# The fourth conv group of a conv + RWKV channel-mix kernel: x instead of the Toeplitz matrix as the stationary operand

## The chip, the cores and the metric

One core of a Trainium2 chip. The metric is the time of one execution on the device, in microseconds (us). Engines: PE (TensorE: matmuls, and PEld, its weight loads), DVE (VectorE), ACT (ScalarE), POOL (GpSimd) and SP (SyncE, DMA issue). PSUM is the memory that matmuls write; SBUF is the one that all engines and DMA use.

## The reference, cut to what matters

A causal 7-tap convolution along the sequence, one set of softmaxed taps for each of 8 heads of 24 channels, and then the RWKV channel mix on its output y (8 sequences of 4160 tokens, 192 channels, d_ff 1024):

```python
# convolution: w = softmax(weight) per head, x padded with 6 zero rows in front
out = np.einsum('hk,bskhg->bshg', w, x_unf)
# channel mix, on x = out
x_prev = np.concatenate([np.zeros((B, 1, D), dtype=np.float32), x[:, :-1, :]], axis=1)
xk = mu_k * x + (1.0 - mu_k) * x_prev
xr = mu_r * x + (1.0 - mu_r) * x_prev
k = np.maximum(xk @ w_k, 0.0)
v = k * k @ w_v
r = 1.0 / (1.0 + np.exp(-(xr @ w_r)))
return (r * v).astype(np.float32)
```

## The kernel before, in words

The sequences are worked in four pairs. The channel mix wants y with channels on the partitions: tile yT, 128 partitions of 3 channel thirds of 64 channels, the pair's two sequences one above the other. The convolution of a block of tokens is a matmul with a banded Toeplitz matrix of a head, `toe[:, h, :]`, built from the taps at the start.

The channel mix runs in steps of 512 tokens of a pair (the first of 256). Each step has d = y - y_prev, xk and xr on DVE (lines 530 to 571), then for each 128 columns of d_ff one *slot*: k_mm (six matmuls into a PSUM tile of two banks, line 591), k_relu on ACT into k_sb (line 603), k_square on DVE into k2 (line 617). Four slots make a *bundle*. Later r (line 648), r_out (a sigmoid on ACT, line 659), v_rows (64 matmuls with wv in two halves, line 679) and v_out (r times v on DVE, line 695, then stored by SP) finish 256 tokens.

All PSUM is one ring of four tiles of two banks, tag "k": the k tiles, ps_r, ps_v and the convolution's tiles (ps_c, ps_t) take turns, and a new one waits until the engine that reads the oldest free one is done. After the first v half a `clobber_nop` stands on ACT, which lets the second half write the banks in the other order.

The order is written out by hand: every engine runs its instructions in the order of the code (`manual_schedule`). The first bundles have a function each: `bundle_first` (bundle 0), `bundle_second` (1), `bundle_third` (2); from bundle 3 on `bundle_rest`. Tables (early, mix_a, mix_b, mix_c, late, xt and so on) name what else runs in a bundle.

The convolution of pair 0 has six groups of tokens. Groups 0, 1 and 2 (3, 4 and 4 blocks of 120 tokens) are done by `conv_t`: x is the stationary operand in 128x32 tiles (126 tokens with their halo by up to 32 channels), `toe` is the moving one with 120 columns, so the result stands with channels on the partitions, and one copy, `to_yT`, takes it to yT. A tile of 32 channels touches two heads, so each (sequence, 32 channels) has two matmuls, the second over the narrower piece. Group 3 (5 blocks, tokens 1320 to 1919; its x is called x3 here) goes another way. In bundle 1 `conv_mm` makes two units of eight matmuls, `toe` stationary in 64x128 tiles; `conv_out` casts them from PSUM into y (tokens on the partitions), the first unit in bundle 1, the second in bundle 2; and in bundle 3 `tr` turns y by 15 transposes with an identity matrix on PE, into two PSUM tiles, from which DVE makes three copies into yT. Groups 4 and 5 of pair 0 and all groups of the other pairs write y to DRAM and read it back with a transposing DMA.

x is loaded by POOL's DMA queue, which casts to bf16: the weights wk, wr and wv come by the same queue. x3 and group 0 to 2 share one buffer `xb`, which group 6 takes over at the head of bundle 3: a small memset on DVE (line 123) waits until the old tile is free, then POOL sets rows to zero (line 125) and issues the loads. POOL also makes the identity `ident` (`select_equal`) in the prologue, between the loads of group 2 and of group 3.

Of the kernel before, what the change touches and what calls it, by code (L numbers as in the profile page):

```python
# [7 lines left out]
FP32 = mybir.dt.float32  # L8
BF16 = mybir.dt.bfloat16
# [5 lines left out]
def kernel(  # L15
# [23 lines left out]
    GB = 10  # L39
# [4 lines left out]
    BANK = 512  # L44
# [3 lines left out]
    YC = 16  # L48
# [31 lines left out]
    n = 0  # L80
# [108 lines left out]
    ident = const.tile([P, P], BF16)  # L189
# [78 lines left out]
    def select_equal(t, n):  # L268
        nc.gpsimd.affine_select(
            out=t,  # L270
            in_=(ones_t if t is ident else ones6)[0:n, 0:n],
            pattern=[[1, n]],
            compare_op=ALU.is_equal,
            fill=0.0,
            base=0,
            channel_multiplier=-1,
        )
# [94 lines left out]
    def conv_units(g):  # L372

        return [((0, 1), (6, 7)), ((2, 3), (4, 5))]

    def conv_mm(g, c, half):

        nb = groups[g][2]
        if half == 0:
            if c == 0:  # L380
                ys[g] = two.tile([P, GB, 2 * D], BF16, tag="y", name="y")
            conv_ps[g, c] = ring.tile([P, 2, BANK], FP32, tag="k", name="ps_c")
        unit = conv_units(g)[c]
        last = len(unit[0]) - 1
        banks = conv_ps[g, c][:, :, 0 : nb * 2 * G * (last + 1)].rearrange("p i (n s c) -> p i n s c", n=nb, s=2)
        for k in range(last + 1):
            for i in range(2):
                q = slice(i * Q, (i + 1) * Q)
                bank = (i + half) % 2
                h = unit[bank][k]  # L390
                nc.tensor.matmul(
                    out=banks[:, bank, :, :, k * G : (k + 1) * G],
                    lhsT=toe[q, h, :],
                    rhs=xbs[g][q, :nb, :, h * G : (h + 1) * G],
                    start=half == 0 and k == 0,
                    stop=half == 1 and k == last,
                )
        if half == 0:
            nc.scalar.clobber_nop([nc.scalar.lower_ap(conv_ps[g, c])])

    def conv_t(g, c, o, blocks):

        for n, i in enumerate(blocks):
            for first_piece in (True, False):
                for s in range(2):
                    for q in range(2):
                        c0 = c * Q + q * 32
                        lo, hi = c0 // G, (c0 + 31) // G
                        h, m = (hi, 32) if first_piece else (lo, hi * G - c0)
                        p0 = s * Q + q * 32  # L410
                        nc.tensor.matmul(  # L411
                            out=o[p0 : p0 + m, n * BLK : (n + 1) * BLK],
                            lhsT=xbs[g][:, i, s, c0 : c0 + m],
                            rhs=toe[:, h, 0:BLK],
                            start=True,
                            stop=True,
                        )

# [3 lines left out]

    def conv_out(g, c, copy):

        nb = groups[g][2]
        unit = conv_units(g)[c]
        w = G * len(unit[0])
        ps = conv_ps.pop((g, c))[:BLK, :, :]
        y = ys[g][:BLK, :, :]
        parts = []  # L430
        for hs in unit:
            c0, c1 = hs[0] * G, (hs[-1] + 1) * G
            cuts = [c0] + [a for a in range(Q, D, Q) if c0 < a < c1] + [c1]
            parts.append(sorted((b - a, a - c0, a // Q * 2 * Q + a % Q) for a, b in zip(cuts, cuts[1:])))
        for (n, s0, d0), (m, s1, d1) in zip(*parts):
            assert n == m and d1 > d0
            copy(
                out=bass.AP(
                    tensor=y.tensor,
                    offset=y.offset + d0,  # L440
                    ap=[y.ap[0], [d1 - d0, 2], [2 * D, nb], [Q, 2], [1, n]],
                ),
                in_=bass.AP(
                    tensor=ps.tensor,
                    offset=ps.offset + s0,
                    ap=[ps.ap[0], [BANK + s1 - s0, 2], [2 * w, nb], [w, 2], [1, n]],
                ),
            )
# [41 lines left out]

    def tr(g, j):

        p, base, nb, _, _ = groups[g]
        ps = ring.tile([P, 2, 2 * BANK], BF16, tag="k", name="ps_t")
        todo = range(4 * j, min(nb, 4 * j + 4))
        view = ps[:, :, 0 : 6 * BLK].rearrange("p b (c i t) -> p b c i t", c=3, i=2)
        for i0 in todo[::2]:
            for c in range(3):
                for i in range(i0, min(nb, i0 + 2)):
                    nc.tensor.transpose(  # L500
                        out=view[:, (i - 4 * j) // 2, c, i % 2, :],
                        in_=ys[g][:BLK, i, c * P : (c + 1) * P],
                        identity=ident[:BLK, :BLK],
                    )

        for i in todo[::2]:
            n = min(2, nb - i)
            c0 = YC + base + i * BLK
            nc.vector.tensor_copy(
                out=yTs[p][:, :, c0 : c0 + n * BLK].rearrange("p c (n t) -> p c n t", n=n),  # L510
                in_=view[:, (i - 4 * j) // 2, :, :n, :],
            )
# [223 lines left out]
    def conv_half(unit, half):
        if unit is not None:
            conv_mm(*unit, half)
            if half == 1:
                conv_out(*unit, nc.scalar.copy)  # L740

    for g, (p, base, nb, fb, on_pe) in enumerate(groups):
        if g < 3:
            continue
        if p == 0:
            xs = {3: [1, 1], 4: [2, 2, 3, 3], 5: [4, 4, 5, 5]}[g]
# [4 lines left out]
        if not on_pe:  # L751
            at(late, xs[-1], y_write, g)
# [10 lines left out]
        if not on_pe:  # L763
            if g == 4:
                at(mix_c, 4, y_read, g, slice(0, 1), 2)
                at(late, 4, y_read, g, slice(1, 2), 2)
            else:
                at(late, 6, y_read, g)
# [54 lines left out]
    def prologue():  # L823
# [38 lines left out]
        select_equal(ident, P)  # L862
# [7 lines left out]
    def bundle_first(ns):  # L870
        new_yT(0)
        tiles = [ring.tile([P, 2, BANK], FP32, tag="k", name="ps_t") for _ in range(2)]
        for n, (g, c) in enumerate((g, c) for g in range(2) for c in range(NC)):
            o = tiles[n % 2][:, n // 2 % 2, :]
            conv_t(g, c, o, range(groups[g][2]))
# [24 lines left out]
    def bundle_second(b, ns):  # L900
# [15 lines left out]
        conv_t(g, 2, outs[2], range(4))  # L916
# [14 lines left out]
    def bundle_rest(b, ns):  # L931
# [3 lines left out]
        if b == 3:  # L935
# [3 lines left out]
            tr(3, 0)  # L939
            tr(3, 1)  # L940
# [42 lines left out]
    def bundle_third(b, ns):  # L983
# [13 lines left out]
        conv_out(*xt[b - 1][1], nc.scalar.copy)  # L997
# [67 lines left out]
```

## Time and profile before

| | us |
|---|---|
| three runs | 411.59, 412.29, 415.82 |
| median | 412.29 |
| span of the profiled execution, first to last instruction | 409.5 |
| sixteen conv matmuls of group 3 start (bundle 1) | 18.74 |
| first v pass starts (bundle 2) | 22.60 |
| fifteen transposes start (bundle 3) | 27.94 |

No time of its own is listed for the profiled execution beside its span; the median of the runs is 2.8 us longer than that span.

In a row of the timeline stand start, length, engine, line, operation, out<-in, the shape of the tile and of the data, and the count of merged instructions. Matmuls are pipelined, so lengths of neighbouring groups overlap and the difference of two starts is what a group takes. In brackets is the time that the engine was idle before, and what ended it. "issue" means that the profile shows nothing that was waited for.

### The profile page before, as it was taken

The page shows a single profiled execution, that of the slowest core. Times are in us where ns is not written, and L with a number is a line of the kernel's source. Part 1 is how long each engine was busy: PE and PEld are TensorE (multiplying, and loading weights), DVE is VectorE, ACT ScalarE, POOL GpSimd, SP SyncE. Part 2 cuts the span into 40 slices and gives each one's busy share as a digit, 9 for nine tenths or more (in the row PEclk, how much of TensorE's full clock was granted, in tenths as well). Part 3 has the DMA queues.
Part 4 walks back from the last instruction along what each step waited for, and adds up shares of the span by engine and source line. Part 5 has one row for each costly group of instructions (what it writes and reads, how often), then busy time and mean ns, then how long its engine had stood idle before and what let it go on. Part 6 is the DMA issues. An engine that isn't in the chain of part 4 may idle for free.

```text
span 409.5 us, 17547 instructions
## 1 busy us (share of the span) xinstructions
PE 401.2 (98%) x7736; PEld 302.2 (74%) x7736; DVE 370.4 (90%) x672; ACT 354.6 (87%) x426; POOL 56.8 (14%) x91
## 2 busy tenths in 40 slices
PE   8899999999999999999999999999999999999996
PEld 5567777777877767777776777777777778777795
DVE  5999898988999989999999999999999899999973
ACT  6899989989888989988898998889899878877781
POOL 8622202200230202004020022000000000000000
PEclk9999999999999999999999999999999999999999
DMA  9999999997399998789995996977623856221223
GB/s 148 188 201 207 197 204 192 213 249 179 90 203 264 193 193 134 158 212 178 205 141 151 236 170 132 171 176 206 121 91 89 209 135 157 80 71 48 80 80 115
DMA packets 138955, 66.23 MB, mean 162 GB/s; under 512 B 89356, under 2 KB 138880, under 8 KB 138880
## 3 DMA queue, kind: packets, MB, share of 16 engines
q1 hardware_dynamic: 95536, 48.20, 46.9%
q0 software_dynamic: 42544, 16.36, 34.8%
q8 instruction: 60, 0.98, 0.9%
q10 hardware_dynamic: 800, 0.57, 0.5%
q14 instruction: 15, 0.12, 0.1%
HBM read 33.29 MB, written 36.86 MB: 171 GB/s over the span
## 4 chain that ended last, share of the span: by engine, by line
PE 92%; DMA 4%; POOL 1%; DVE 1%; ACT 1%; issue 1%; POOLq 0%; DVEq 0%
PE ps_v L679 41%; PE ps_k L591 39%; PE ps_r L648 8%; PE ps_c L362 2%; DMA xb<-in_x_dram 2%; DMA wk<-in_moe_w_k_dram 2%; PE ps_v L631 1%; ACT k_sb L603 1%; PE ps_c L317 0%; POOL wk L224 0%; POOL xb L152 0%; DVE k L617 0%; DVE yT L421 0%; DVE o_sb L695 0%; POOL tap L258 0%
## 5 line engine op out<-in xcount | busy, mean ns | idle before, releaser
L603 ACT ACTIVATE k_sb<-ps_k 128x1024 bf16<-128x1024 f32 x260 | 253.3, 1038 | 34.9 <-PE ps_k L591 33.8
L617 DVE TENSOR_TENSOR k<-k_sb 128x1024 bf16<-128x1024 bf16 x260 | 173.6, 688 | 26.1 <-ACT k_sb L603 25.8
L591 PE MATMUL ps_k<-xk,wk 64*128 64x512 bf16 (+1 forms) x1632 | 192.0, 367 | 1.5 <-DMA wk<-in_moe_w_k_dram 1.3
L679 PE MATMUL ps_v<-wv,k 64*128 64x192 bf16 x4032 | 188.5, 243 | 0.5 <-DMA wv<-in_moe_w_v_dram 0.5
L679 PEld LDWEIGHTS <-k 64*128 64x128 bf16 x4032 | 168.2, 94 | 13.1 <-issue 4.6
L591 PEld LDWEIGHTS <-wk 64*128 64x128 bf16 x1632 | 83.6, 94 | 56.9 <-issue 2.0
L695 DVE TENSOR_TENSOR o_sb<-ps_v,r_sb 128x768 f32<-128x768 f32 x64 | 60.9, 951 | 2.6 <-issue 2.4
L152 POOL DMA_DIRECT2D xb<-in_x_dram x62 | 43.5, 708 | 131.8 <-DVE xb L111 59.8
L659 ACT ACTIVATE r_sb<-ps_r 128x768 bf16<-128x768 f32 x65 | 53.4, 824 | 7.9 <-PE ps_v L679 5.7
L335 ACT CAST y<-ps_c 128x960 bf16<-128x960 f32 (+2 forms) x84 | 52.6, 708 | 0.0
L648 PEld LDWEIGHTS <-xr 64*128 64x128 bf16 x780 | 35.0, 94 | 14.8 <-issue 1.0
L648 PE MATMUL ps_r<-wr,xr 64*128 64x192 bf16 x780 | 43.4, 243 | 0.3 <-issue 0.3
L565 DVE TENSOR_SCALAR xr<-d,mu 128x512 bf16<-128x512 bf16 (+1 forms) x102 | 35.2, 349 | 0.0
L565 DVE TENSOR_SCALAR xk<-d,mu 128x512 bf16<-128x512 bf16 (+1 forms) x99 | 32.5, 358 | 0.1
L534 DVE TENSOR_TENSOR d<-yT 128x1536 bf16<-128x1536 bf16 (+4 forms) x36 | 31.2, 867 | 1.2 <-ACT yT L421 1.1
L571 DVE TENSOR_TENSOR xr<-xr,yT 128x1536 bf16<-128x1536 bf16 (+1 forms) x33 | 31.1, 941 | 1.1
L571 DVE TENSOR_TENSOR xk<-xk,yT 128x1536 bf16<-128x1536 bf16 (+3 forms) x33 | 30.5, 925 | 0.1
L518 POOL COPY y_tail<-yT 128x195 bf16<-128x195 bf16 x4 | 2.8, 690 | 89.1 <-DMA yT<-y_dram 89.1
L362 PEld LDWEIGHTS <-toe 32*32 32x32 bf16 x768 | 4.9, 87 | 10.2 <-issue 8.7
L362 PE MATMUL ps_c<-xb,toe 32*32 32x240 bf16 x768 | 10.7, 267 | 0.0
L125 POOL MEMSET xb<- 32x384 bf16 x3 | 1.2, 407 | 67.1 <-DVE xb L123 67.1
L411 PE MATMUL ps_t<-toe,xb 128*32 128x120 bf16 (+3 forms) x264 | 5.4, 234 | 0.3 <-ACT yT L421 0.2
(60 smaller groups left out, 61.8 us busy)
## 6 DMA issues: line engine op xcount, KB each, us to landing
out_dram<-o_sb SPq DMA_DIRECT2D x128, 192.0 KB
xb<-in_x_dram POOLq DMA_DIRECT2D x52, 240.0 KB, 8.1
y_dram<-y SPq DMA_DIRECT2D x48, 195.0 KB
y_dram<-y SPq DMA_DIRECT2D x8, 210.0 KB
xb<-in_x_dram POOLq DMA_DIRECT2D x6, 228.0 KB, 4.7
xb<-in_x_dram POOLq DMA_DIRECT2D x4, 192.0 KB, 6.5
wk<-in_moe_w_k_dram POOLq DMA_DIRECT2D x4, 192.0 KB, 6.2
wv<-in_moe_w_v_dram POOLq DMA_DIRECT2D x1, 384.0 KB, 10.1
```

What stands on the lines that cost most here:

```text
L152: nc.gpsimd.dma_start(out=xb[q0 : q0 + rows, lo:hi, s, :], in_=bass.AP(tensor=x.tensor, offset=x.offset + (b * S + t0 + lo * step) * D, ap ...
L335: nc.scalar.copy(out=bass.AP(tensor=y.tensor, offset=y.offset + d, ap=[y.ap[0], [m * 2 * D, 2], [2 * D, m], [Q, 2], [1, b - a]],), in_=bas ...
L534: nc.vector.tensor_tensor(out=shaped(s, diffs[s][:, cs, :L]), in0=y_of(s, cs, 1), in1=y_of(s, cs, 0), op=ALU.subtract)
L565: nc.vector.tensor_scalar(out=t[:, c, :L], in0=diffs[s][:, c, :L], scalar1=mu[:, i, c : c + 1], scalar2=None, op0=ALU.mult)
L571: nc.vector.tensor_tensor(out=o, in0=o, in1=y_of(s, sl, 0), op=ALU.add)
L591: nc.tensor.matmul(out=ps[:, i, f * L : (f + 1) * L], lhsT=wk[r, c, fs], rhs=xk[r, c, :L], start=c == 0 and f == 0, stop=c == NC - 1 and f ...
L603: nc.scalar.activation(out=k_sb, in_=ps.rearrange("p a b -> p (a b)"), func=AF.Relu)
L617: nc.vector.tensor_tensor(out=o, in0=i, in1=i, op=ALU.mult)
L648: nc.tensor.matmul(out=ps[:, i, k * D : (k + 1) * D], lhsT=xr[q, c, ts], rhs=wr[q, c, :], start=c == 0, stop=c == NC - 1,)
L659: nc.scalar.activation(out=r_sbs[s, j], in_=r_ps.pop((s, j))[:, :, 0 : 2 * D], func=AF.Sigmoid)
L679: nc.tensor.matmul(out=v_ps[s, j][:, bank, k * D : (k + 1) * D], lhsT=k2s[s][q, f, t * P : (t + 1) * P], rhs=wv[q, f, :], start=half == 0 ...
L695: nc.vector.tensor_tensor(out=o_sb.rearrange("p (b t) d -> p b (t d)", b=2), in0=v_ps.pop((s, j)), in1=r_sbs.pop((s, j)), op=ALU.mult,)
```

## The change

Group 3 is done by `conv_t` too. It takes a list of pieces (block, first column, end column) instead of blocks. The new `conv_t5` does one channel third of five blocks: two and a half blocks into each of a PSUM tile's two banks, the third block in halves of 60 columns, and one cast of 600 columns into yT, by ACT for thirds 0 and 1 and by DVE for third 2. Third 0 runs in bundle 1, third 1 in bundle 2 behind the first v pass, third 2 in bundle 3 where the transposes were. `conv_units`, `conv_mm`, `conv_out`, `conv_half`, `tr` and `ident` go.

```diff
-        select_equal(ident, P)
...
+    def conv_t(g, c, o, pieces):
+
+        at = 0
+        for i, t0, t1 in pieces:
...
-                            out=o[p0 : p0 + m, n * BLK : (n + 1) * BLK],
+                            out=o[p0 : p0 + m, at : at + t1 - t0],
                             lhsT=xbs[g][:, i, s, c0 : c0 + m],
-                            rhs=toe[:, h, 0:BLK],
+                            rhs=toe[:, h, t0:t1],
                             start=True,
                             stop=True,
                         )
+            at += t1 - t0
...
+    def conv_t5(g, c, copy):
+
+        ps = ring.tile([P, 2, BANK], FP32, tag="k", name="ps_t")
+        h = BLK // 2
+        conv_t(g, c, ps[:, 0, :], [*whole(2), (2, 0, h)])
+        conv_t(g, c, ps[:, 1, :], [(2, h, BLK), (3, 0, BLK), (4, 0, BLK)])
+        c0 = YC + groups[g][1]
+        copy(
+            out=yTs[0][:, c, c0 : c0 + 5 * BLK].rearrange("p (b t) -> p b t", b=2),
+            in_=ps[:, :, 0 : 5 * h],
+        )
...
         run(mix_a, b)
-        conv_half(xt[b][0], 0)
         k_relu(ns[3])
-        conv_half(xt[b][0], 1)
+        conv_t5(3, 0, act_)
         k_square(ns[1])
         run(mix_b, b)
-        conv_mm(*xt[b][1], 0)
-        conv_mm(*xt[b][1], 1)
         run(mix_c, b)
...
-            tr(3, 0)
-            tr(3, 1)
+            conv_t5(3, 2, nc.vector.tensor_copy)
...
         v_rows(*quad, 0)
-        conv_out(*xt[b - 1][1], nc.scalar.copy)
+        conv_t5(3, 1, nc.scalar.copy)
         k_square(ns[1])
```

How it moves instructions. PE in bundle 2, at the end of the first v pass: before, the k pass follows at once.

```order
L679 LDWEIGHTS k_504
L679 MATMUL ps_v<-wv,k_504 128x192
L591 LDWEIGHTS wk
L591 MATMUL ps_k<-xk,wk 128x512 [waits Activation_49]
L591 LDWEIGHTS wk
```

Now the 48 matmuls of third 1 start there, with x as the weights (the line numbers are those of the changed kernel).

```order
L616 LDWEIGHTS k_502
L616 MATMUL ps_v<-wv,k_502 128x192
L382 LDWEIGHTS xb
L382 MATMUL ps_t<-toe,xb 32x120 [waits Activation_49]
L382 LDWEIGHTS xb
```

The k pass stands behind all 48; in bundle 1 the sixteen ps_c matmuls are gone, and 48 of these stand in the place of the first four.

ACT in bundles 1 and 2 before: the relu of bundle 1's last slot, the cast of the first unit, two relus, the sigmoid, the second unit's two casts.

```order
L603 ACTIVATE k_sb<-ps_k 128x1024 [waits DVE_49,Activation_49,PE_49]
L437 CAST y<-ps_c 120x2x5x2x48 [waits Activation_sequencer_49,PE_49]
L603 ACTIVATE k_sb<-ps_k 128x1024 [waits Activation_49,PE_49,DVE_49]
L603 ACTIVATE k_sb<-ps_k 128x1024 [waits DVE_49,PE_49]
L659 ACTIVATE r_sb<-ps_r 128x768 [waits PE_49]
L437 CAST y<-ps_c 120x2x5x2x16 [waits Activation_49,PE_49,Activation_sequencer_49]
L437 CAST y<-ps_c 120x2x5x2x32
```

And now:

```order
L540 ACTIVATE k_sb<-ps_k 128x1024 [waits PE_49,Activation_49]
L401 CAST yT<-ps_t 128x600 [waits PE_49]
L540 ACTIVATE k_sb<-ps_k 128x1024 [waits DVE_49,PE_49] x2
L596 ACTIVATE r_sb<-ps_r 128x768 [waits PE_49]
L401 CAST yT<-ps_t 128x600 [waits DVE_49,Activation_49,PE_49]
```

Three casts into y have become two into yT, at the same places among the relus.

DVE at the head of bundle 3 before: v_out of bundle 2, the memset that takes the old x buffer for group 6, the three copies of the transposes, two squares.

```order
L695 TENSOR_TENSOR o_sb<-ps_v,r_sb 128x768 [waits Activation_sequencer_49,PE_49,Activation_49]
L123 MEMSET xb 1x1 [waits DMASW6_49,DMASW7_49,DMASW1_49,DMASW0_49]
L509 COPY yT<-ps_t 128x3x240 [waits PE_49]
L509 COPY yT<-ps_t 128x3x240
L509 COPY yT<-ps_t 128x3x120 [waits PE_49]
L617 TENSOR_TENSOR k_644<-k_sb 128x1024 [waits Activation_49] x2
```

And now:

```order
L632 TENSOR_TENSOR o_sb<-ps_v,r_sb 128x768 [waits Activation_sequencer_49,PE_49,Activation_49]
L123 MEMSET xb 1x1 [waits DMASW6_49,DMASW1_49,DMASW7_49,DMASW0_49,PE_49]
L401 CAST yT<-ps_t 128x600
L554 TENSOR_TENSOR k_642<-k_sb 128x1024 [waits Activation_49] x2
L502 TENSOR_SCALAR xr<-d,mu 128x512 x3
```

The memset has gained a wait for PE, since third 2 is the last reader of x3, and the cast behind it needs no wait of its own any more.

More of the change, by code (lines that the diff above doesn't have):

```diff
@@ L188 @@
     ones_t = const.tile([P, P], BF16)
-    ident = const.tile([P, P], BF16)
     w_nrm = const.tile([32, 32], BF16)
@@ L270, in select_equal @@
             out=t,
-            in_=(ones_t if t is ident else ones6)[0:n, 0:n],
+            in_=ones6[0:n, 0:n],
             pattern=[[1, n]],
@@ L370, in conv_sparse @@
             cast_tiles(y, ps, m, c)
[L372 to L403, printed above, removed]
+    def conv_t(g, c, o, pieces):
+        at = 0
+        for i, t0, t1 in pieces:
             for first_piece in (True, False):
@@ L417, in conv_t, with whole @@
                         )
+            at += t1 - t0
+    def whole(n):
+        return [(i, 0, BLK) for i in range(n)]
+    def conv_t5(g, c, copy):
[8 more added lines that the diff above has]
+        )
     def to_yT(g, c, o, b0, b1, copy):
@@ L421, in to_yT @@
         copy(out=yTs[0][:, c, c0 : c0 + (b1 - b0) * BLK], in_=o[:, 0 : (b1 - b0) * BLK])
[L423 to L448, printed above, removed]
     def new_yT(p):
@@ L488, in y_read @@
         )
[L491 to L512, printed above, removed]
     diffs, xks, xrs = {}, {}, {}
@@ L734, in at @@
         table.setdefault(b, []).append((fn, a))
[L736 to L740, printed above, removed]
     for g, (p, base, nb, fb, on_pe) in enumerate(groups):
-        if g < 3:
+        if g < 4:
             continue
         if p == 0:
-            xs = {3: [1, 1], 4: [2, 2, 3, 3], 5: [4, 4, 5, 5]}[g]
+            xs = {4: [2, 2, 3, 3], 5: [4, 4, 5, 5]}[g]
         else:
@@ L750 @@
             xt.setdefault(b, []).append((g, i))
-        if not on_pe:
-            at(late, xs[-1], y_write, g)
+        at(late, xs[-1], y_write, g)
         if g in sparse:
@@ L762 @@
             continue
[L763 to L768, printed above, removed]
+        if g == 4:
+            at(mix_c, 4, y_read, g, slice(0, 1), 2)
+            at(late, 4, y_read, g, slice(1, 2), 2)
+        else:
+            at(late, 6, y_read, g)
         if g > 4:
@@ L874, in bundle_first @@
             o = tiles[n % 2][:, n // 2 % 2, :]
-            conv_t(g, c, o, range(groups[g][2]))
+            conv_t(g, c, o, whole(groups[g][2]))
             if n == 0:
@@ L908, in bundle_second @@
         outs = [tiles[0][:, 0, :], tiles[1][:, 0, :], tiles[0][:, 1, :]]
-        conv_t(g, 0, outs[0], range(4))
+        conv_t(g, 0, outs[0], whole(4))
         to_yT(g, 0, outs[0], 0, 4, dve_)
         k_relu(ns[1])
-        conv_t(g, 1, outs[1], range(4))
+        conv_t(g, 1, outs[1], whole(4))
         to_yT(g, 1, outs[1], 0, 4, dve_)
@@ L915, in bundle_second @@
         k_relu(ns[2])
-        conv_t(g, 2, outs[2], range(4))
+        conv_t(g, 2, outs[2], whole(4))
         to_yT(g, 2, outs[2], 0, 4, act_)
```

## The prediction

> **What bounds the kernel now.** I read the page first (busy time per engine), then stretches of the span, then TensorE's waits, then the timeline of bundles 1 to 3, where all changed instructions lie. The page's first part, and four stretches (each engine's busy us, granted clock, busy share of the DMA engines, GB/s):
>
> ```profile
> PE 401.2 (98%) x7736; PEld 302.2 (74%) x7736; DVE 370.4 (90%) x672; ACT 354.6 (87%) x426; POOL 56.8 (14%) x91
> ...
> 18.50:22.60 4.10, 3.37 (x44) 2.04 (x41) 4.07 (x9) 3.95 (x6) 2.16 (x4) 1.00 1.59 191
> 22.60:29.40 6.80, 6.64 (x114) 4.77 (x115) 6.18 (x13) 6.01 (x9) 1.40 (x3) 1.00 1.59 192
> 29.40:46.00 16.60, 16.58 (x308) 11.95 (x311) 16.33 (x31) 16.06 (x22) 4.05 (x7) 1.00 1.18 215
> ```
>
> TensorE is the bound from 22.6 us on (6.64 of 6.80, 16.58 of 16.60 us), at a granted clock of 1.00. Before that it is not: 3.37 of 4.10 us. DVE and ACT run close behind it up to 46 us. TensorE's waits from 29 us to the end:
>
> ```profile
> PE ps_r L648 <- issue: 0.3, 1, 0.3
> PE ps_k L591 <- issue: 0.2, 1, 0.2
> PE ps_c L317 <- ACT k_sb L603: 0.2, 1, 0.2
> ```
>
> 0.7 us in 380. So a delay of TensorE at 29 us is a delay of the end: no idle time is left to absorb it. The timeline of TensorE in bundles 1, 2 and 3 (start, length, what, count; bracketed, the idle time before it and its releaser):
>
> ```profile
> 15.73 1.02 PE L411 MATMUL ps_t<-toe,xb 128*32 128x120 bf16 x64
> 16.80 0.82 PE L591 MATMUL ps_k<-xk,wk 64*128 64x512 bf16 x6
> 17.55 0.60 PE L411 MATMUL ps_t<-toe,xb 128*32 128x120 bf16 x32
> 18.09 0.82 PE L591 MATMUL ps_k<-xk,wk 64*128 64x512 bf16 x6
> 18.74 1.52 PE L391 MATMUL ps_c<-xb,toe 64*128 64x240 bf16 x16
> 20.09 1.47 PE L591 MATMUL ps_k<-xk,wk 64*128 64x512 bf16 x12
> 21.38 0.68 PE L648 MATMUL ps_r<-wr,xr 64*128 64x192 bf16 x12
> 22.60 1.49 PE L679 MATMUL ps_v<-wv,k 64*128 64x192 bf16 x32 [0.55 <-DMA wv<-in_moe_w_v_dram]
> 23.93 0.81 PE L591 MATMUL ps_k<-xk,wk 64*128 64x512 bf16 x6
> 24.58 0.82 PE L679 MATMUL ps_v<-wv,k 64*128 64x192 bf16 x16
> ...
> 26.55 1.46 PE L591 MATMUL ps_k<-xk,wk 64*128 64x512 bf16 x12
> 27.94 0.96 PE L500 MATMUL ps_t<-ident,y 120*128 120x120 bf16 x15
> 28.83 0.40 PE L317 MATMUL ps_c<-xb,toe 64*64 64x240 bf16 x8
> 29.39 0.40 PE L317 MATMUL ps_c<-xb,toe 64*64 64x240 bf16 x8 [0.16 <-ACT k_sb L603]
> 29.81 0.82 PE L591 MATMUL ps_k<-xk,wk 64*128 64x512 bf16 x6
> ```
>
> The reader is to take differences of starts, since the lengths overlap: 16 v matmuls cost 0.66 us, a k pass of six 0.65, the 15 transposes 0.89. The one real wait lies at 22.60: the first v pass needs wv, and TensorE stands 0.55 us for its transfer. Work taken off TensorE ahead of that point buys nothing; work added behind it is paid in full.
>
> **The change, part by part.** First the price of one new convolution: 48 matmuls in 128x32 tiles, 32 of them 120 columns wide and 16 of them 60. The same instruction with 120 columns stands in the timeline: 64 take 1.07 us (15.73 to 16.80), 32 take 0.54 (17.55 to 18.09), so 16.8 ns each, with no fixed part. The 60-column form does not occur before. Its bounds are no saving (16.8 ns) and half (8.4 ns), so a channel third costs 0.67 to 0.81 us; the nearest rows decide for neither end, and I take the middle, 0.74. Entering the narrow tiles costs a little: the k pass ahead of them steps 0.75 us (16.80 to 17.55) against 0.65 ahead of a v pass, so 0.10; leaving them costs nothing that shows.
>
> The page "TensorEngine Tiling (Array Packing)" of the Trainium skill (Instruction Overhead) puts about 60 cycles under each matmul, so that 60 columns would not yet be padded; by it the 60-column form costs half and a third 0.67 us. Its section Key Properties says that a change of tiling mode drains the array, which speaks against this change, as it adds one such excursion in bundle 2; the trace agrees that there is a cost and makes it 0.10 us.
>
> *Bundle 1, the sixteen L391 matmuls (both units) replaced by one third:* 1.35 us (18.74 to 20.09) goes, 0.74 + 0.10 comes: TensorE is 0.51 us earlier at 22.60, where it now stands about 1.06 us for wv instead of 0.55. On the path: 0, hidden by that wait; were the wait gone, it would be worth its 0.51. Whether wv can come earlier depends on POOL and the DMA:
>
> ```profile
> 8.27 0.37 POOL L269 TENSOR_SCALAR_AFFINE_SELECT ident<-ones_t 128x128 bf16<-128x128 bf16 x1
> ...
> 12.20 0.93 POOL L237 DMA_DIRECT2D wv<-in_moe_w_v_dram  x1 [0.34 <-DMA wk<-in_moe_w_k_dram]
> ...
> 22.57 0.71 POOL L152 DMA_DIRECT2D xb<-in_x_dram  x1 [1.84 <-DMA wv<-in_moe_w_v_dram]
> ```
>
> The identity's select goes from POOL, and x3 and wr are issued up to 0.37 us sooner. But wv's own issue at 12.20 waited for wk to land, and the transfer took until 22.5 with the DMA engines full (share 1.59). Bounds for its gain: 0 to 0.37 us; I take 0, as that row names a landing and not POOL.
>
> The other engines in bundles 1 to 3, and the first reader of group 6's x:
>
> ```profile
> 20.20 0.95 ACT L437 CAST y<-ps_c 120x960 bf16<-120x960 f32 x1
> ...
> 22.86 0.84 ACT L659 ACTIVATE r_sb<-ps_r 128x768 bf16<-128x768 f32 x1
> ...
> 24.21 1.02 ACT L437 CAST y<-ps_c 120x320 bf16<-120x320 f32 x2 [0.50 <-ACTq L687]
> ...
> 27.28 0.95 DVE L695 TENSOR_TENSOR o_sb<-ps_v,r_sb 128x768 f32<-128x768 f32 x1
> 27.40 1.94 ACT L603 ACTIVATE k_sb<-ps_k 128x1024 bf16<-128x1024 f32 x2 [0.28 <-PE ps_k L591]
> ...
> 28.17 0.06 DVE L123 MEMSET xb<- 1x1 uint32 x1
> ...
> 28.40 0.41 POOL L125 MEMSET xb<- 32x384 bf16 x1 [5.11 <-DVE xb L123]
> ...
> 28.78 1.22 DVE L509 COPY yT<-ps_t 128x720 bf16<-128x720 bf16 x3 [0.55 <-PE ps_t L500]
> ...
> 29.92 1.28 DVE L617 TENSOR_TENSOR k<-k_sb 128x1024 bf16<-128x1024 bf16 x2
> ...
> 57.86 0.42 PE L362 MATMUL ps_c<-xb,toe 32*32 32x240 bf16 x32
> ```
>
> *Bundle 2, the second third put behind the first v pass:* +0.74 + 0.10 = +0.84 us on the path. Its PSUM slot is given back by ACT; even r's is free when r_sb is done at 23.70 (22.86 + 0.84), and the v pass runs to 23.93. Its own cast on ACT takes the place of the two at 24.21.
>
> *Bundle 3, transposes replaced by the last third:* -0.89 + 0.74 = -0.15 us. The switch stays: the k passes ahead of the transposes step 1.39 (26.55 to 27.94) against twice 0.65.
>
> *One PSUM slot less in bundle 3* (one tile for two): the second conv unit takes the first relu's slot, not the second's. The step 28.83 to 29.39 is 0.56 us for matmuls that take 0.42 (29.39 to 29.81): -0.14, bounds -0.16 and 0.
>
> The cast durations (last two numbers: us in all, mean ns):
>
> ```profile
> L421 ACT CAST yT<-ps_t 128x480 bf16<-128x480 f32 x4 | 2.2, 557 | 0.5 <-PE ps_t L411 0.3
> ...
> L421 ACT CAST yT<-ps_t 128x360 bf16<-128x360 f32 x3 | 1.3, 461 | 0.5 <-PE ps_t L411 0.5
> ...
> L421 DVE CAST yT<-ps_t 128x480 bf16<-128x480 f32 x2 | 1.2, 648 | 0.0
> ```
>
> *ACT:* 0.95 + 1.02 us of casts into y go, two casts of 600 come, about 0.65 each (557 plus 120 columns at the 0.8 ns that 557 and 461 give): -0.66. Off the path, hidden under TensorE's matmuls; the relus wait for TensorE instead, which brings them later in bundle 3.
> *DVE:* three copies, 1.14 us from 28.78 to 29.92, become one cast of 600, at most 0.81 (648 times 600/480). But the memset ahead of it now waits for the last read of x3, at the end of the last third. DVE's squares then start 27.94 + 0.84 + 0.74 + some 0.1 + 0.81 = 30.4, 0.5 us later than 29.92. TensorE's v pass that needs them is later by the same 0.55, so 0. Queued behind the memset on POOL stand its memset and the five loads of group 6: from 28.40 to about 29.9. Their first reader is the pass at 57.86, so 0, with 28 us in hand.
>
> Sum: 0 + 0.84 - 0.15 - 0.14 = **+0.55 us**. The span of 409.5 becomes 410.1. The three runs have a median of 412.29, 2.8 us over the span; on that scale **412.8 us**.
>
> **Rivals.** *(a) A small gain.* ACT and DVE, not TensorE, pace 22 to 46 us through PSUM slots (16.06 and 16.33 of 16.60 us busy), so their 0.66 us shows, or wv lands 0.37 us sooner. For: those shares. Against: TensorE's waits on ACT are 0.2 us in all. Time 412.29 - 0.66 = 411.6; with wv alone 412.8 - 0.37 = 412.5.
> *(b) Lag that adds up.* ACT's relus of bundle 3 start 0.84 late, more than TensorE's 0.55, and DVE's squares 0.5 late; with so little idle there a slot comes late once per bundle. Three bundles at 0.4 to 0.6 us add 1.2 to 1.8 to the forecast: 414.0 to 414.6. Against: ACT stood 0.28 us for TensorE at 27.40, so it was not behind.
> *(c) Clearly slower.* The narrow weight loads do not pipeline behind the wide passes:
>
> ```profile
> L411 PEld LDWEIGHTS <-xb 128*32 128x32 bf16 x132 | 3.8, 106 | 1.8 <-issue 1.5 <-ACT xb L245 0.3
> ```
>
> With 106 ns exposed, the 96 matmuls behind wv cost 10.2 us for 0.89 and 0.14: 421. It passes 1% (4.1 us, about what a measurement here can tell from no change) from 53 ns a matmul. Against: 64 of them went by at 16.8 ns with the same loads.
>
> **How the numbers follow.** The forecast, 0 to +1.4 us (both thirds at 0.81 + 0.20, no slot gain, 0.3 of lag), has 0.66; (a) 0.21; (b) 0.10; (c) 0.03. The lowest two runs differ by 0.7 us, which the ends take in: 412.29 - 0.3 - 0.7 = 411.3, and 412.29 + 1.4 + 0.6 = 414.3; outside are (c), most of (b) and the far end of (a). All priced cases but (c) lie within 1%; of (a) 0.02 is kept for a gain that no row prices. So: faster by over 1% 0.02, within 0.95, slower 0.03.
>
> **What would show it.** Right: the wv wait grows to about 1.06 us; 48 matmuls behind the first v pass step 0.7 to 0.8 us; the k pass at 29.81 starts near 30.36; no wait of TensorE after that beyond 0.7 us; DVE idles some 1.2 us before its memset. Wrong: v starting clearly before 22.5; steps over 1 us for a third; new waits of TensorE on ACT or DVE between 30 and 46 us.

## The result and the profile after

| | before | after |
|---|---|---|
| median of 15 runs each (us) | 411.59 (410.71 to 415.82) | 415.11 (414.13 to 417.65) |
| span of the profiled execution (us) | 409.5 | 413.1 |
| mean granted TensorE clock of that execution | 1.000 | 0.996 |

The changed kernel takes 1.0089 times as long, with a 95% interval of 1.0069 to 1.0110. One run in this study (416.99 us, of e10 below) is over 1.5% above the fastest of its kernel and is counted in no ratio. Forecast was 412.8 us with a range of 411.3 to 414.3: the sign was right, the size was not, and the 3.6 us between the two spans has to be found.

TensorE's waits in the changed kernel come first (line, releaser; us in all, times, longest):

```profile
PE ps_t L382 <- issue: 2.7, 1, 2.7
...
PE ps_k L528 <- DMA wk<-in_moe_w_k_dram: 1.0, 2, 0.5
...
PE ps_k L528 <- ACT k_sb L540: 0.2, 1, 0.2
```

The wait for wv, 0.55 us before and forecast to grow to 1.06, has gone. In its place stands one wait of 2.7 us inside the narrow matmuls, and its releaser is "issue": the profile shows nothing that TensorE waited for. The timeline of TensorE puts it into bundle 1 (start, length, what, count, and in brackets the idle time before):

```profile
18.64 0.82 PE L528 MATMUL ps_k<-xk,wk 64*128 64x512 bf16 x6
19.39 0.65 PE L382 MATMUL ps_t<-toe,xb 128*32 128x120 bf16 x41
22.79 0.29 PE L382 MATMUL ps_t<-toe,xb 128*32 128x120 bf16 x7 [2.74 <-issue]
23.00 1.98 PE L528 MATMUL ps_k<-xk,wk 64*128 64x512 bf16 x12
24.78 1.17 PE L585 MATMUL ps_r<-wr,xr 64*128 64x192 bf16 x12
25.74 2.21 PE L616 MATMUL ps_v<-wv,k 64*128 64x192 bf16 x32
27.88 0.71 PE L382 MATMUL ps_t<-toe,xb 128*32 128x120 bf16 x48
28.53 0.82 PE L528 MATMUL ps_k<-xk,wk 64*128 64x512 bf16 x6
...
31.15 1.46 PE L528 MATMUL ps_k<-xk,wk 64*128 64x512 bf16 x12
32.54 0.71 PE L382 MATMUL ps_t<-toe,xb 128*32 128x120 bf16 x48
33.18 0.60 PE L316 MATMUL ps_c<-xb,toe 64*64 64x240 bf16 x16
33.99 0.82 PE L528 MATMUL ps_k<-xk,wk 64*128 64x512 bf16 x6 [0.20 <-ACT k_sb L540]
```

Third 0 is cut after 41 of its 48 matmuls, all of one tile. No buffer can be the reason, since the 42nd writes the tile and reads the data of the 41st. Behind the cut the passes are long: twelve k matmuls step 1.78 us (23.00 to 24.78) where before they stepped 1.29 (20.09 to 21.38), and the first v pass 2.14 (25.74 to 27.88) against 1.33. The stretches of the changed kernel say why (busy us of PE, PEld, DVE, ACT and POOL, then the granted clock, the busy share of the DMA engines, GB/s):

```profile
20.00:22.80 2.80, 0.06 (x5) 0.02 (x5) 2.80 (x6) 0.61 (x1) 2.01 (x3) 1.00 1.63 184
22.80:24.50 1.70, 1.70 (x19) 0.80 (x21) 0.94 (x3) 1.29 (x2) 0.00 (x0) 0.80 1.62 189
24.50:27.00 2.50, 2.50 (x32) 2.08 (x29) 1.61 (x4) 2.16 (x3) 0.00 (x0) 0.50 1.61 196
27.00:29.00 2.00, 2.00 (x74) 1.48 (x72) 1.93 (x5) 0.35 (x1) 0.00 (x0) 0.94 1.57 184
```

After the stop the granted clock goes to 0.50 and is back at 1.00 by 29 us; before, it was 1.00 in all these stretches. The account from there, before against after:

- The k pass behind the first v pass starts at 28.53, and started at 23.93: +4.60. That is 0.19 for the later end of the standstill (22.79 against 22.60), 1.99 for work that stood ahead of it and now stands behind it (7 narrow matmuls 0.21, twelve k 1.29, r 0.49), 1.77 for the half clock (0.49 + 0.47 on k and r, 0.81 on v), and 0.65 for third 1. Some 0.1 of the 0.81 belongs to the change itself: at full clock a v pass ahead of a third steps 1.42 in e10 and 1.43 in e8 below, against 1.33.
- Third 2 steps 0.64 (32.54 to 33.18) where the transposes took 0.89: -0.25. The two conv units step 0.81 (33.18 to 33.99), before 0.98 (28.83 to 29.81): -0.17.
- So the pass at 29.81 now starts at 33.99: +4.18. About 0.5 is won back later, where the two "issue" waits of before (0.3 on L648 and 0.2 on L591) are absent. Spans: +3.6.

The change's own convolution work comes to +0.23 (0.65 - 0.25 - 0.17), or +0.33 with that 0.1. The rest is the standstill and its echo.

**Where the standstill comes from.** The page's table of DMA queues has a row that the prediction never read (packets, MB, share of 16 engines):

```profile
PE 403.0 (98%) x7848; PEld 304.3 (74%) x7849; DVE 370.2 (90%) x670; ACT 354.3 (86%) x425; POOL 56.3 (14%) x90
...
q8 instruction: 61, 1.00, 1.0%
```

61 packets carry 1.00 MB, so 16 KB each; TensorE has 7848 + 7849 = 15,697 matmuls and weight loads, and 1.00 MB over these is about 64 bytes apiece. So q8 brings TensorE its program, 256 instructions to a packet. Counting TensorE's instructions in the trace one by one, its few semaphore and drain instructions among them (five up to here), the cut in third 0 stands after 960 of them. Up to 35 us the unexplained stands of the other kernels lie, give or take one, at the same counts, 449, 705, 961, 1217 and 1473 (steps of 256), whatever instruction is there. The two waits of the kernel before on "issue" that the prediction lists, at 82.5 us (L591) and 147.6 us (L648), are at counts 3265 and 5825, on the same steps. The next lines are worked out from the starts of all instructions and packets in the traces (the experiments follow below): when TensorE issues the first instruction of a block, when the next q8 packet starts, when it has come to the block's end, and when it goes on.

```
kernel                block  entered  next packet  at its end  goes on
before                  705    15.96     20.12        21.81      22.60
after                   705    16.52     19.89        19.83      22.78
e1_after_minus64        193     6.54     10.84         9.07      13.19
e1_after_minus64        705    20.89     24.06        25.60      26.58
e3_before_plus64        705    14.50     18.40        19.39      20.68
e5_before_dummies       705    16.42     19.64        20.27      21.97
e6_after_gated          705    15.65     18.86        19.10      21.16
e6_after_gated          961    21.16     25.10        26.23      27.45
e8_after_third0_late    961    21.54     25.12        24.54      27.46
e9_before_dummies16     705    15.88     19.58        21.12      22.27
e12_after_thirds_late  1217    28.14     29.78        31.11      32.11
e10_after_fewer         705    15.92     18.90        21.98    no stand
```

The lines agree on a rule. The packet with the next block starts some 3.0 to 4.3 us after TensorE has entered the block ahead of it, between 6 and 27 us, while the weights and x are loaded (DMA share about 1.6 in most of these kernels), and 1.6 us after it in e12 at 28 us; TensorE can use it 2.3 to 2.9 us after its start. Over all blocks of the fourteen traces none was entered sooner than 2.19 us after its packet had started. So in that stretch a block must hold 5.5 to 6.7 us of work, or TensorE stands for the rest. Block 705 held 5.85 us of work before (15.96 to 21.81), and holds 3.31 now (16.52 to 19.83): the sixteen ps_c matmuls in it were wide and few, 32 instructions in 1.35 us, and the third is 96 in half that time.

The first line is the lesson of this case: the one wait of the kernel before that the prediction rested on, 0.55 us for wv at 22.60, lies at count 961 too. By the trace's semaphore records wv had landed at 22.29, and the pass started 0.31 us after that; in e8 and e10 below, where its start is no border, it follows wv's landing by 0.04 and 0.05 (20.90 to 20.94, 21.34 to 21.39). So two causes ended close together there, and the profile named the one that ended first.

The Trainium skill, "Runtime: NRT & Kernel Launch" (Instruction fetch mechanics), says that instruction memory is refilled in blocks of 16 KiB and that crossing a block border is mostly hidden. The trace agrees on the block; the crossing cost 2.74 us here.

### The profile page after: what moved, and what is told of

It reads as the page before. It is cut to its first block, busy times and chain, and to the rows that moved or that the text cites. A ratio compares the mean times of both kernels' runs of the same rounds, so it can differ in the third digit from the quotient of the medians.

```text
span 413.1 us, 17764 instructions
## 1 busy us (share of the span) xinstructions
PE 403.0 (98%) x7848; PEld 304.3 (74%) x7849; DVE 370.2 (90%) x670; ACT 354.3 (86%) x425; POOL 56.3 (14%) x90
## 4 chain that ended last, share of the span: by engine, by line
PE 94%; DMA 2%; issue 1%; POOL 1%; ACT 1%; DVE 0%; POOLq 0%; DVEq 0%; ACTq 0%
PE ps_v L616 41%; PE ps_k L528 40%; PE ps_r L585 8%; PE ps_c L361 2%; DMA wk<-in_moe_w_k_dram 2%; PE ps_v L568 1%; PE ps_t L382 1%; ACT k_sb L540 1%; POOL wk L223 0%; POOL xb L152 0%; PE ps_c L316 0%; DVE o_sb L632 0%; POOL tap L257 0%; DVE o_sb L652 0%; DVE xr L502 0%
## 5 line engine op out<-in xcount | busy, mean ns | idle before, releaser
L361 PEld LDWEIGHTS <-toe 32*32 32x32 bf16 x768 | 5.0, 87 | 10.2 <-issue 8.7
L382 PE MATMUL ps_t<-toe,xb 128*32 128x120 bf16 (+6 forms) x408 | 8.4, 242 | 3.2 <-issue 2.7
L382 PEld LDWEIGHTS <-xb 128*32 128x32 bf16 (+3 forms) x408 | 6.7, 107 | 5.7 <-issue 4.8
```

## The experiments

Two theories stood against each other. F: TensorE's program arrives in blocks at a bounded rate while the DMA engines are loaded, and the change puts more instructions into that stretch than arrive. N: the new work itself costs it, by its narrow matmuls and weight loads, x3's later release or the PSUM slots. The ratios are to the kernel before on the same chip.

**Shifting the borders.** Where a border falls can be moved without touching the work: the prologue has matmuls that only keep TensorE warm and whose results nobody reads. The first three kernels change their number and width so that their time stays nearly the same: 64 instructions fewer ahead of the changed kernel's bundles, 128 fewer, and 64 more in the kernel before.

```diff
 e1, changed kernel
-    SHORT = 78
-    FILL = (6, 3)
+    SHORT = 44
+    FILL = (8, 3)
 e2, changed kernel
-    WARM = (3, 2)
-    SHORT = 78
+    WARM = (4, 2)
+    SHORT = 13
 e3, kernel before
-    SHORT = 78
-    FILL = (6, 3)
+    SHORT = 112
+    FILL = (4, 3)
```

> The changed kernel with 64 fewer TensorE instructions in the prologue (34 fewer short warm-up pairs, two more filling ones). Theory F (instruction supply): TensorE runs out of instructions at its 960th recorded one, where a 16 KB block ends, and stands until the next block is there, at about 22.7 us. Then the break moves 64 instructions on in the program, to the third matmul of the first v pass, which TensorE reaches at about 21.9: the stop shrinks from 2.74 us to under 1 us, no half clock follows, 48 matmuls of third 0 run in one piece. The next break falls into the k passes of bundle 3 and may bring a stop of about 1 us. Time 1 to 3 us under the changed kernel: 412 to 414. Theory N (the narrow matmuls themselves, x3's transfer, or a PSUM slot hold TensorE): the stop stays behind the 41st matmul of third 0, 2.7 us, and the time stays at 415.

Measured: 416.81 us, ratio 1.0139 (1.0095 to 1.0182). Its timeline of TensorE:

```profile
7.81 1.48 PE L382 MATMUL ps_t<-toe,xb 128*32 128x120 bf16 x65
13.19 0.58 PE L382 MATMUL ps_t<-toe,xb 128*32 128x120 bf16 x15 [3.91 <-issue]
...
23.23 0.71 PE L382 MATMUL ps_t<-toe,xb 128*32 128x120 bf16 x48
...
31.28 0.60 PE L528 MATMUL ps_k<-xk,wk 64*128 64x512 bf16 x4
33.60 1.04 PE L528 MATMUL ps_k<-xk,wk 64*128 64x512 bf16 x8 [1.73 <-issue]
```

Third 0 runs in one piece, as F expected. The time does not get better, against F's number: TensorE now stands earlier, at count 449 in the convolution of group 0 (3.91 us), then for under 1 us at 961, and again at 1217, in the middle of a k pass. A longer half clock comes with the stand at 449: the granted clock is 0.52 from 12 to 14 us and 0.50 from 14 to 18. With fewer and wider instructions ahead it enters block 193 at 6.54 us instead of 4.59, and the first packet of q8 starts at 10.84 instead of 6.63. The places follow the count and the packets follow the entry; shifting does not make the time shorter.

> The changed kernel with 128 fewer TensorE instructions in the prologue (65 fewer short warm-up pairs, one more long one). F: the break moves into the first matmuls of third 1, reached after 23 us, when the block is there: no stop in bundles 1 and 2 but for wv (landed at 21.85 in the changed kernel), so the first v pass starts near 21.9. The following break falls into third 2 in bundle 3, reached at 28.4, the block there at about 29.2: a stop of at most 1 us. Time 411 to 412.5. N: as the changed kernel, 415.

Measured: 417.01 us, ratio 1.0157 (1.0109 to 1.0204): a miss for the time again. First packet at 11.74, stands at 449 (12.84 to 14.20) and 961 (26.50 to 27.25), third 0 in one piece. Here too the clock is halved, 0.53 from 12 to 14 us and 0.50 from 14 to 18; that begins ahead of the stand at 449, behind waits for wk of 0.95 and 1.30 us.

> The kernel before with 64 more TensorE instructions in the prologue (34 more short warm-up pairs, two fewer filling ones), nothing of the change. F: the break moves back to about the twelfth of the sixteen ps_c matmuls of bundle 1, reached at 19.6; TensorE stands there some 3 us, until 22.7, in runs where the idle time is long enough at half clock afterwards. Time 3 to 4.5 us over the kernel before: 414.5 to 416. N: same as before, 411.6.

Measured: 413.08 us, ratio 1.0034 (1.0004 to 1.0063), under the number expected. The place is the one expected, though: in the kernel before, which has no narrow fourth group, the sixteen ps_c matmuls are cut at count 961.

```profile
18.81 0.85 PE L391 MATMUL ps_c<-xb,toe 64*128 64x240 bf16 x8
20.68 0.85 PE L391 MATMUL ps_c<-xb,toe 64*128 64x240 bf16 x8 [1.03 <-ACT k_sb L603]
```

The profile names ACT as releaser here, for a relu that ended at 20.38. But in the kernel before the same sixteen matmuls run through without a stop while that relu is still at work (19.28 to 20.31), so they do not need it. The packet started 2.28 us ahead of the ninth, at 18.40. With 64 more instructions ahead TensorE enters block 193 at 2.28 us, so that all packets come earlier too (4.35, 12.13, 18.40); hence the small cost.

**Relieving the DMA engines.** Group 4's load of x moves out of the prologue into bundle 1, and group 5's into bundle 2.

```diff
 e4, changed kernel
-            at(mix_a, 1, x_tile, g)
-            at(mix_a, 1, load_x, g)
+            at(mix_a, 1, x_tile, 4)
+            at(mix_a, 1, load_x, 4)
+            at(mix_b, 2, x_tile, g)
+            at(mix_b, 2, load_x, g)
...
-        x_tile(4)
-        load_x(4)
```

> The changed kernel with the load of group 4's x moved from the prologue to bundle 1 and that of group 5 from bundle 1 to bundle 2, so that fewer x packets are queued while the block is fetched. F with a fetch that is slowed by the full DMA engines: the stop shrinks from 2.74 us to under 1.5 us, time 411.5 to 413.5. F with a fetch time of its own: the stop stays near 2.7 us and the time near 415. N: near 415.

Measured: 415.66 us, ratio 1.0121 (1.0068 to 1.0175), with the same 2.7 us stand. It says little about the stand, since POOL ran the loads ahead all the same and the DMA share stayed 1.63 from 20 to 23 us. Behind it, though, the share fell to 1.49 and then 0.25, and the packet after block 961 was entered (22.78) started 1.21 us later, at 23.99; in the changed kernel, with a share of 1.6, it took 3.95 (22.78 to 26.73). So the next pair also ties these loads to a memset on DVE (`if g > 3` for `if g > 4` at the memset of x's buffer), in the changed kernel (e6) and in the one before (e7).

> The changed kernel with group 4's x load held back by a memset on DVE in bundle 1 (about 18.2 us) and group 5's by one in bundle 2 (about 25): unlike in the earlier try the loads can't run ahead, so the DMA engines are free from about 18 us at the latest. F with a fetch slowed by the full DMA: the block for the 961st instruction comes sooner, the stop of 2.74 us shrinks to under 1 us, wv lands before 20, no half clock. Time 411 to 413. F with a fetch time of its own (6.5 us whatever the load): stop as before, 414 to 416. N: 415.

Measured: 415.55 us, ratio 1.0111 (1.0085 to 1.0136). Stretches of this kernel, columns as above, and its timeline:

```profile
18.00:20.00 2.00, 1.32 (x47) 0.61 (x47) 1.97 (x8) 1.89 (x3) 1.56 (x3) 1.00 0.95 110
20.00:22.00 2.00, 0.84 (x13) 0.42 (x15) 2.00 (x4) 0.51 (x1) 1.29 (x2) 1.00 1.06 117
22.00:24.00 2.00, 2.00 (x40) 1.60 (x38) 1.72 (x4) 1.91 (x3) 0.00 (x0) 1.00 1.50 177
```

```profile
21.16 0.28 PE L382 MATMUL ps_t<-toe,xb 128*32 128x120 bf16 x7 [1.84 <-issue]
...
27.45 0.42 PE L616 MATMUL ps_v<-wv,k 64*128 64x192 bf16 x6 [0.98 <-issue]
```

The stand shrank from 2.74 to 1.84 us and the clock stayed 1.00, but the packet came 3.21 us after block 705 was entered (15.65 to 18.86), in the changed kernel 3.37. This says nothing against the load of the DMA engines: while the packet was awaited the share was still 1.59 up to 18 us and 1.43 from there to 18.86, and it fell to 0.55 only as the packet started. The second cut is a new stand at 1217, and group 6's x came late (a new wait of 1.5 us at L361). The time did not come down.

> The kernel before with the same two loads held back. F with a fetch slowed by the DMA: the stop of 0.55 us at the first v pass goes, and wv lands sooner: 410.3 to 411.3. Fixed fetch time: no change, 411.2.

Measured: 413.99 us, ratio 1.0065 (1.0040 to 1.0090), a miss for the time: putting the loads off costs by itself (1.8 us for group 6's x at L362, and 3.4 us of half clock behind that wait). The stop at the first v pass did go, as F expected: the pass starts at 22.84 after 0.08 us of idling. The packet came 2.95 us after block 705 was entered (16.67 to 19.62), against 4.16 before, and the DMA share had fallen to 0.77 by then. So F's explanation by the load of the DMA engines has some support, from this and from e4's 1.21 against 3.95 us, and no proof.

**The slowdown without the change.** e5 is the kernel before with 32 matmuls of one column put ahead of the first ps_c unit, into a corner of its tile that the unit overwrites: 64 instructions and next to no work. e9 has 16 of them.

```diff
+            for i in range(32 * (c == 0)):
+                q = slice(i % 4 * 32, i % 4 * 32 + 32)
+                nc.tensor.matmul(
+                    out=conv_ps[g, c][q, 0, 0:1], lhsT=ones_t[:, 0:32], rhs=ones_t[:, 0:1], start=True, stop=True
+                )
```

> The kernel before with 32 tiny matmuls (one column each, results overwritten) put ahead of the first ps_c unit of bundle 1: 64 TensorE instructions more at that place and 0.3 us of work, the prologue unchanged. F (TensorE is out of instructions at its 961st recorded one until the next block has come through the full DMA): the stop moves from the first v pass back into the sixteen ps_c matmuls, starts at about 20 us and lasts until about 22.7, 2.5 to 3 us; k, r and the first v pass follow late. Time 2.5 to 4.5 us over the kernel before: 413.7 to 415.7. N (the narrow conv matmuls themselves cost the time): the 0.3 us of the tiny matmuls, hidden at the wv wait: 411 to 412.

Measured: 415.51 us, ratio 1.0101 (1.0065 to 1.0136). Timeline of TensorE:

```profile
19.29 0.36 PE L385 MATMUL ps_c<-ones_t 128*32 128x1 bf16 x32
19.59 0.94 PE L396 MATMUL ps_c<-xb,toe 64*128 64x240 bf16 x9
21.97 0.85 PE L396 MATMUL ps_c<-xb,toe 64*128 64x240 bf16 x7 [1.44 <-issue]
22.64 2.63 PE L596 MATMUL ps_k<-xk,wk 64*128 64x512 bf16 x12
25.03 1.20 PE L653 MATMUL ps_r<-wr,xr 64*128 64x192 bf16 x12
25.99 1.61 PE L684 MATMUL ps_v<-wv,k 64*128 64x192 bf16 x32
```

This is the clearest run. The dummies take 0.30 us (19.29 to 19.59), and the kernel loses 4 us: a stand at count 961 in the middle of a unit, twelve k matmuls in 2.39 us (the granted clock is 0.50 from 24 to 26 us), and the first v pass at 25.99, where the changed kernel has it at 25.74. Convolution, x3 and PSUM slots are those of before, which N would have left at the time of before.

> The kernel before with 16 tiny matmuls instead of 32 ahead of the first ps_c unit: half the dose, 32 TensorE instructions. F: the 961st instruction now lies in the k passes ahead of r, reached at about 21; TensorE stands there until about 22.5, and what it has not done by then (the rest of the k passes, r) comes late, about 1.3 us; the idle time is mostly too short for a half clock. Time 1 to 2 us over the kernel before: 412.2 to 413.2. N: 411.2 to 411.5.

Measured: 412.39 us, ratio 1.0017 (0.9994 to 1.0041). The stand is at count 960, now inside the k passes (`[0.78 <-issue]`, 21.12 to 22.27), and v starts at 23.0. The clock was not halved, and the loss cannot be told from none. So half of the dummies cost a small part of what all cost: it is a threshold and not a price per instruction, since block 705 then ends inside the k passes and holds 5.24 us of work (15.88 to 21.12), with 32 dummies only 3.85.

**Moving the new work.** In e8 third 0 moves from bundle 1 to bundle 2, ahead of third 1.

```diff
-        conv_t5(3, 0, act_)
...
         v_rows(*quad, 0)
+        conv_t5(3, 0, nc.scalar.copy)
         conv_t5(3, 1, nc.scalar.copy)
```

> The changed kernel with third 0 moved from bundle 1 to bundle 2, right ahead of third 1 (96 narrow matmuls in a row behind the first v pass). F: the 961st instruction now lies in the middle of the first v pass, reached after 22.3, so that stop shrinks to under 0.7 us; but the next block holds both thirds and is used up by about 25.8, while it takes until 29 for the following one: a new stop of 2.5 to 3.5 us at the 1217th instruction, in the second half of v. Time 414 to 417. N (x3's transfer or a slot in bundle 1 holds third 0): no stop, 412 to 413.

Measured: 415.27 us, ratio 1.0098 (1.0059 to 1.0137), as F expected.

```profile
20.94 1.50 PE L616 MATMUL ps_v<-wv,k 64*128 64x192 bf16 x32 [0.60 <-DMA wv<-in_moe_w_v_dram]
22.37 1.24 PE L382 MATMUL ps_t<-toe,xb 128*32 128x120 bf16 x96
23.54 0.82 PE L528 MATMUL ps_k<-xk,wk 64*128 64x512 bf16 x6
24.20 0.58 PE L616 MATMUL ps_v<-wv,k 64*128 64x192 bf16 x10
27.46 0.42 PE L616 MATMUL ps_v<-wv,k 64*128 64x192 bf16 x6 [2.68 <-issue]
```

The reader is to see two things. Without third 0 ahead of it the first v pass starts at 20.94, right at wv's landing (20.90), which is itself 1.39 us earlier than in the kernel before; the border at 961 now lies inside the pass and costs nothing. And all 96 narrow matmuls go by in 1.17 us, 12 ns each, while the stand has moved behind the tenth v matmul after them, count 1217.

**Fewer instructions.** e10 and e11 leave out the same work from both kernels, the second piece of each tile of 32 channels in group 2's convolution (48 matmuls, 96 instructions, all ahead of the place).

```diff
-            for first_piece in (True, False):
+            for first_piece in (True, False)[: 1 if g == 2 else 2]:
```

> The changed kernel without the 48 second pieces of group 2's convolution in bundle 1 (left out, so some channels of tokens 840 to 1319 are convolved with the wrong head's taps): 96 TensorE instructions fewer ahead of the thirds, 0.4 us less work, all of the change in place. F: the 961st instruction lies in the first v pass, reached after 22, when its block is about there: the stop of 2.74 us and the half clock go; the next border lies in third 2, reached at about 28, a stop of at most 1.2 us. Time 411.5 to 413. N: the change costs as before, 414.6 to 415.1.

> The control: the kernel before without the same 48 second pieces. F: the first v pass is still bound by wv's landing at about 22.5, so the 0.4 us of work does not show: 410.6 to 411.4. N: 0.4 us less at most, the same range.

Measured: e10 413.12 us over all ten runs and 412.82 over the nine that its ratio counts, 1.0040 (1.0009 to 1.0071), at the upper end of F's range; e11 411.14 us, ratio 0.9999 (0.9980 to 1.0018), as expected. What leads to it is not as expected: in e11 wv lands at 20.32, and the first v pass starts at 21.63 and not at 22.5. In e10's profiled execution TensorE has no stand at all around the three thirds:

```profile
18.58 0.71 PE L382 MATMUL ps_t<-toe,xb 128*32 128x120 bf16 x48
19.22 1.47 PE L528 MATMUL ps_k<-xk,wk 64*128 64x512 bf16 x12
...
21.39 1.49 PE L616 MATMUL ps_v<-wv,k 64*128 64x192 bf16 x32 [0.20 <-DMA wv<-in_moe_w_v_dram]
22.81 0.71 PE L382 MATMUL ps_t<-toe,xb 128*32 128x120 bf16 x48
...
27.47 0.71 PE L382 MATMUL ps_t<-toe,xb 128*32 128x120 bf16 x48
28.11 0.60 PE L316 MATMUL ps_c<-xb,toe 64*64 64x240 bf16 x16
28.93 0.82 PE L528 MATMUL ps_k<-xk,wk 64*128 64x512 bf16 x6 [0.21 <-ACT k_sb L540]
```

In the control e11:

```profile
21.63 1.50 PE L679 MATMUL ps_v<-wv,k 64*128 64x192 bf16 x32
...
28.94 0.82 PE L591 MATMUL ps_k<-xk,wk 64*128 64x512 bf16 x6
```

All the new work is there, and the k pass behind it starts at 28.93, in e11 at 28.94: with the supply in order, the change is worth nothing either way at that point. Both are 0.9 us ahead of the kernel before (29.81), and the spans, 409.9 and 409.5, are no shorter than its 409.5: each now waits for group 6's x (1.45 us at L361 and 0.91 at L362, a difference of 0.54). The counted runs lie further apart, by 1.7 us in the median. Among e10's nine counted runs the three with a mean clock of 0.996 average 414.4 us and the other six 412.4; so it looks as if the stand and the half clock come back in some of its runs. No such run was profiled, and this stays open.

**A better place for the new work.** Last, all three thirds behind the crowded stretch: third 0 at the end of bundle 2, thirds 1 and 2 together in bundle 3.

```diff
-        conv_t5(3, 0, act_)
...
+            conv_t5(3, 1, nc.scalar.copy)
             conv_t5(3, 2, nc.vector.tensor_copy)
...
-        conv_t5(3, 1, nc.scalar.copy)
...
         v_rows(*quad, 1, (1,))
+        conv_t5(3, 0, nc.scalar.copy)
         v_out(*quad)
```

> The changed kernel with its thirds placed later: third 0 at the end of bundle 2 (behind the last v half), thirds 1 and 2 together in bundle 3 ahead of the conv units; all of the computation is there. F (instruction supply): without third 0 in bundle 1 the 961st instruction falls into the first v pass, which starts near 20.9 us with no stop; the 1217th is the ninth matmul of third 1, reached near 27.0 us while its block comes near 27.5, so the stop is 0 to 0.6 us, and the k pass behind the conv units starts 29.0 to 29.6 (29.81 before). Clock 1.00. Time 0.3 to 0.8 us under the kernel before, at worst equal: ratio 0.997 to 1.001. N (the narrow matmuls, x3's memset or the PSUM slots cost the time): they are all there, so the ratio stays 1.007 to 1.011, as for the changed kernel.

Measured: 413.57 us, ratio 1.0050 (1.0031 to 1.0068): between F's number and N's, so it missed both. Its timeline:

```profile
21.76 0.84 PE L616 MATMUL ps_v<-wv,k 64*128 64x192 bf16 x16 [0.42 <-issue]
...
28.07 1.24 PE L382 MATMUL ps_t<-toe,xb 128*32 128x120 bf16 x96 [0.65 <-DVE o_sb L632]
29.25 0.60 PE L316 MATMUL ps_c<-xb,toe 64*64 64x240 bf16 x16
29.79 0.82 PE L528 MATMUL ps_k<-xk,wk 64*128 64x512 bf16 x6
...
30.94 0.41 PE L616 MATMUL ps_v<-wv,k 64*128 64x192 bf16 x6
32.11 1.25 PE L616 MATMUL ps_v<-wv,k 64*128 64x192 bf16 x26 [0.76 <-issue]
```

The k pass behind the conv units starts at 29.79, as early as before (29.81), in spite of a PSUM slot that DVE gave back 0.65 us late. But the surplus of instructions was not gone: the next border, 1473, which the expectation had not looked at, cost a stand from 31.11 to 32.11, and 410.9 against 409.5 is the span. Placed so, the change loses a good half of what it lost (1.0050 instead of 1.0089), and the kernel before stays the fastest of all.

## Why the prediction missed

The step that failed is the first term of the sum: "On the path: 0, hidden by that wait". It weighed bundle 1 in microseconds, 1.35 of ps_c matmuls going and 0.84 coming, and found TensorE 0.51 us early at a wait. In instructions it is 16 matmuls going and 48 coming, 64 more with their weight loads, ahead of a border at count 961. Behind that term stood the reading that "the first v pass needs wv, and TensorE stands 0.55 us for its transfer". That was one of two causes: wv had landed at 22.29, and the pass started at 22.60, on a border. The slack that the term rests on was there for wv but not for the instructions. The stand took the place of the wait, moved 1.99 us of work behind it, ended 0.19 later, and brought 1.77 us of half clock (1.67 if the switch to the narrow tiles is taken out), for which the sum had no term: 3.95 us. e5 loses as much without any of the change's own work.

Point by point:

- Third 1 behind the first v pass: forecast +0.84, measured 0.65 (27.88 to 28.53; 0.65 in e10 too) and about 0.10 for entering, which shows in the v pass ahead of it (1.42 in e10 for 1.33). The 60-column halves cost about half, where the sum took the middle.
- Third 2 for the transposes: forecast -0.15, measured -0.25. PSUM slot: forecast -0.14, measured -0.17. With third 1 these make +0.33 where the sum had +0.55.
- ACT and DVE: right that their changes stay off the path. ACT's only wait that TensorE felt there is the 0.20 at 33.99, and it was 0.16 before.
- POOL and group 6's x: no wait for it in the changed kernel, as forecast, but not with 28 us in hand. The last load of group 6 is issued behind a later memset on DVE (L111), at 47.56 in the kernel before, and landed at 57.38, half a microsecond ahead of the pass at 57.86. In e10 and e11, where TensorE is earlier, it is late. That load does not hang on x3's release, which the change moved.
- Rival (a), ACT and DVE pacing: not seen. With the casts gone and no stand, e10's k pass is no earlier than e11's. Rival (b), a lag that adds up: the size was nearly right by accident, but no slot came late. Rival (c), narrow weight loads exposed: 96 matmuls in 1.17 us exclude it.
- None of the rivals had the instruction supply, and the prediction's own marks would have pointed to it: the wv wait did not grow but vanished.

The half clock does not follow each stand. In the profiled executions it came after 2.74 us of idling here, after 2.72 in e4 and 1.44 in e5, and within the 3.91 of e1, and not after 1.84 in e6 or 2.68 in e8. Over the changed kernel's 15 runs, the six with a mean clock of 1.000 average 414.6 us, the nine with 0.990 to 0.996 average 416.2: 1.6 us, close to the 1.77 read from the trace. Without it the change would have stood some 3 us over the kernel before.

What stays open: why a packet waits 3 to 4 us after a block is entered. e4 and e7 point to the load of the DMA engines and e6 cannot tell; in e12 a packet came after 1.64 us at a share of 1.50, so the share alone does not set it, and no run varied the load alone. And e10's scatter.

## What to carry to other kernels

Count instructions and not only microseconds where many small matmuls meet heavy loads: here each 256 instructions of TensorE had to hold 5.5 to 6.7 us of work, 22 to 26 ns apiece, and a swap that saves time but adds instructions lost several times its gain. A wait whose releaser lands at the very end may have a second cause that ends at the same time; see whether its instruction count lies a multiple of 256 from another unexplained stop before its time is spent as slack. A stop in the middle of a group that writes one tile and reads one buffer is no data dependency, whatever name stands beside it.

## What the hardware showed that was not expected

- TensorE's program arrives as 16 KB packets on a queue of its own (61 packets for 15,697 instructions), about one block ahead at most: up to 33 us each packet started only after the block ahead of it was entered, and later none started more than 1.3 us before that. The Trainium skill gives TensorE room for 2048 instructions in the section named above; in these traces it never had as much ahead, as it stood for the block that it was about to enter.
- Fewer instructions in the prologue made it worse: with 64 fewer TensorE stood 3.91 us at count 449, while the changed kernel passes it without a stop.
- The half clock came after stands of 1.44 and 2.74 us, and within one of 3.91. The Trainium skill, "TensorE: Matmul & The Clock Gate" (Part 1: The HAM clock gate), puts the idle window at about 3.4 us and says that it runs freely, so that the moment varies. The trace agrees that it varies (1.84 and 2.68 us left the clock at 1.00), but shorter stands than a window were enough.
- 128x32 tiles go by fast with their weight loads: 96 matmuls, two thirds of them 120 columns and one third 60, in 1.17 us at full clock.
